# ScalarE's queue in the seven-product down layers: program order in place of the scheduler's order

## The chip, the cores and the metric

The kernel runs on one NeuronCore of one Trainium2 chip. The metric is device time of one execution in microseconds (us). Three runs of the kernel before gave 905.02, 900.41 and 902.4 us: a median of 902.4.

The engines are named as the profile names them: PE is TensorE (matmul) and PEld its weight loads, DVE is VectorE, ACT is ScalarE, POOL is GpSimd, SP is the engine that issues most of the DMAs. Each engine works off its own queue of instructions, and semaphores hold an instruction back until what it needs is done.

## The reference

Two stages, in float32. First an attention within chunks of 64 positions (batch 8, 8 heads, 576 positions, head dimension 64): for every chunk, `softmax(q k^T / 8) v`. The result is laid out as `x` with 4608 tokens of 512 features. Then a gated feed-forward layer:

```
gate = 1 / (1 + exp(-(x @ w_gate)))     # 512 -> 1536
val  = x @ w_val                        # 512 -> 1536
out  = (gate * val) @ w_out             # 1536 -> 512
```

## The kernel before

The 4608 tokens are nine blocks of 512. Float32 operands are split in two float32r parts, a high part (a cast on ACT) and a low part (value minus high part, on DVE); each product then takes three matmuls (weight high with data high, weight high with data low, weight low with data high), always in this order.

Blocks 0 to 2 go through plain up and down layers. The other six blocks go in three pairs, n = 0, 1, 2. A pair is computed as a 2 by 2 block product with seven products in place of eight (a Winograd form), once for the up layers (`first`, `middle`, `last`, lines 518 to 568) and once for the down layer (`down_begin`, `down_products`, lines 644 to 718). Blocks 1 and 2 share the down layer too, as pair n = -1.

A down layer walks through 42 spots: seven products r in the order 1, 6, 2, 7, 5, 4, 3, with six slices f each (`SPOTS`, line 573). A spot is six matmuls of 512 columns. Before its matmuls run, its data must be split: `down_split` (lines 625 to 642) casts the high part on ACT (line 640, into tiles `hs` and `hx`) and subtracts the low part on DVE (line 641). Splits are issued three spots ahead in pairs -1, 0 and 1, and six ahead in pair 2. Spots 0, 1 and 4, 5 and so on lie two to a tile `hs` of which there is one; spots 2, 3 and 6, 7 and so on lie in two tiles `hx`. So the cast of spot q + 4 has to wait until the matmuls of the spots that used the same tile are done.

In between (`between`, lines 928 to 936), with each spot of pairs -1, 0 and 1, the operands of the next pair's up layers are prepared from its attention output `raw` (`operands`, `lower`, lines 476 to 499). There are seven, named B11, B22, T1, T3, B21, T2, T4. For each, ACT casts 1024 columns (`xc`, line 489) and DVE subtracts the low part (line 498). The four named T need a difference of two quarters of `raw` first, made on DVE in place (line 485). The casts of B11, B22 and B21 need no such difference.

The rest of the work in a down layer is the reading of finished banks: on ACT lines 674 and 682, on DVE lines 686 and 689, and the sums for later products on DVE (lines 617 to 621, 705).

What sets the order of an engine's queue: inside `tc.manual_schedule(engines=...)` the named engines take instructions in the order in which the code issues them. Engines that are not named are put in order by a scheduler, which moves an instruction forward or back by its own estimate of when its inputs are there. Lines 942 to 951 name PE, DVE, SP and POOL for all pairs, and ACT for `singles()` and `pair(-1)`.

Of the kernel before, what the change touches and what calls it, by code (L numbers as in the profile page):

```python
# [42 lines left out]
FIRST_PAIR = 3  # L43
# [10 lines left out]
def chunk_attn_moe(ctx: ExitStack, tc: tile.TileContext, q, k, v, w, out, turned_out):  # L54
# [377 lines left out]
    def place(n):  # L432
        rotation.append(rotation.pop(0))
        return wp.tile([P, n], F32R, tag=rotation[-1], name="wr")
# [3 lines left out]
    def load_group(n, p, which, parts=(0, 1)):  # L438

        def of_given(t, n):  # L440
            return lambda a, c: t[:, n * 512 + a * 256 + c * P:n * 512 + a * 256 + (c + 1) * P]
        def of_sums(t, n):
            return lambda a, c: t[:, n * 512 + c * 256 + a * P:n * 512 + c * 256 + (a + 1) * P]
        lhs = groups.setdefault((n, p, which), {})
        for part in parts:
            g, g0, s = ((2, 0, slice(0, 4, 3)), (1, 2, slice(1, 3)))[part]
            t = place((g + 2) * 512)
            if p < RESIDENT:
                nc.sync.dma_start(
                    t[:, :g * 512].rearrange("p (g n) -> p g n", g=g).bitcast(F32),  # L450
                    given[p, which][:, g0:g0 + g].rearrange("p g a n -> p g (a n)"))
            else:
                of_given = of_sums
                for k in range(g):
                    nc.sync.dma_start(
                        t[:, k * 512:(k + 1) * 512].rearrange("p (c a n) -> p c a n", c=2, a=2).bitcast(F32),
                        whole[p, which][:, part, :, (part + k)::2])
            nc.sync.dma_start(
                t[:, g * 512:].rearrange("p (s n) -> p s n", s=2).bitcast(F32),
                sums[p, which][:, s].rearrange("p s c n -> p s (c n)"))  # L460
            if part == 0:
                lhs.update({
                    1: (of_given(t, 0), "B11"), 2: (of_given(t, 1), "B21"), 6: (of_sums(t, 2), "T2"),
                    5: (of_sums(t, 3), "T1")})
            else:
                lhs.update({4: (of_given(t, 0), "T4"), 3: (of_sums(t, 1), "B22"), 7: (of_sums(t, 2), "T3")})
# [36 lines left out]
    def product(n, p, which, r, bank, start, stop):  # L503
        lhs, name = groups[n, p, which][r]
        x, k = xc[n, name], 0
        for c in range(2):
            for wpart, part in ((0, 0), (0, 1), (1, 0)):
                nc.tensor.matmul(  # L508
                    bank, lhsT=lhs(wpart, c), rhs=x[:, part, c], start=start and k == 0, stop=stop and k == 5,
                    skip_group_check=True)  # L510
                k += 1
# [6 lines left out]
    def first(n, p, which):  # L518
        x = ps_o.tile([P, TB], F32, tag="acc", name="cx")
        y = ps_o.tile([P, TB], F32, tag="acc", name="cy")  # L520
        product(n, p, which, 1, x, True, True)
        both = mp.tile([P, 2, TB], F32, tag="hx", name="s1")
        s1, u2 = both[:, 0], both[:, 1]
        nc.scalar.copy(s1, x)  # L524
        product(n, p, which, 6, y, True, True)
        nc.vector.tensor_tensor(out=u2, in0=y, in1=s1, op=ALU.add)  # L526
        banks[n, p, which] = x, y, s1, u2

    def gated(n, f, b, value):

        h = hid[n, f][:, b]
        nc.vector.tensor_tensor(out=h, in0=value, in1=h, op=ALU.mult)
# [21 lines left out]
    def last(n, p, which):  # L554
        y, z, s1, u2 = banks.pop((n, p, which))
        f = 2 * p
        product(n, p, which, 4, y, False, True)
        c21 = hid[n, f + 1][:, 0] if which == 0 else s1
        nc.vector.tensor_tensor(out=c21, in0=y, in1=s1, op=ALU.add)
        product(n, p, which, 3, z, False, True)  # L560
        c12 = hid[n, f][:, 1] if which == 0 else u2
        nc.vector.tensor_tensor(out=c12, in0=z, in1=u2, op=ALU.add)
        if which == 0:
            nc.scalar.activation(hid[n, f + 1], hid[n, f + 1], AF.Sigmoid)
            nc.scalar.activation(hid[n, f][:, 1], hid[n, f][:, 1], AF.Sigmoid)
        else:
            gated(n, f + 1, 0, s1)
            gated(n, f, 1, u2)
# [75 lines left out]
    def down_begin(n):  # L644

        ring["splits"], *ring["weights"] = rotation
        rotation[:] = rotation[4:] + rotation[1:4] + rotation[:1]
        for i in range(2):
            load_down(n, i)
        for q in range(3 if n < LAST else 6):  # L650
            down_split(n, q)
# [136 lines left out]
    def advance():  # L788
        now["unit"] += 2 * (now["item"] == "A")
        now["item"] = next(ahead, None)  # L790
        now["since"] = now["ticks"]

    def tick(share):
        now["ticks"] += 1
        now["credit"] += share
        while now["item"] is not None:
            if isinstance(now["item"], float):
                if now["credit"] < now["item"] / 2:
                    return
                now["credit"] -= now["item"]  # L800
            elif not (now["item"] == "wait" and now["ticks"] > now["since"] + 1
                      or now["item"] == "next" and now["ticks"] > now["since"]
                      or now["item"][0] in ("open", "freed") and now["item"][1] <= now[now["item"][0]]):
                break
            advance()
        now["credit"] = min(now["credit"], share)

    def insert(upto=4 * NB, pieces=0):


        if now["item"] == "S" or (
                now["item"] == "A" and now["unit"] < upto and now["ticks"] >= now["since"] + pieces):
            advance()

    def due(n):

        while now["item"] is not None and len([x for x in xc if x[0] == n]) < 7:
            advance()
# [47 lines left out]
    def keep(n=1):  # L866
        for _ in range(n):
            if kept:
                keep_sums(*kept.pop(0))
# [29 lines left out]
                if kept[0][2] is None:  # L899
                    keep()  # L900

    def pair(n):
        m0 = FIRST_PAIR + 2 * n
        upto = 4 * (m0 + 4)
        order = [(p, which) for p in range(6) for which in range(2)]
        if n >= 0:
            due(n)
        for i, (p, which) in enumerate(order if n >= 0 else ()):
            if i + 1 < len(order) and i > 0:
                load_group(n, *order[i + 1])  # L910
            first(n, p, which)
            tick(SHARES["up"])
            if i:
                keep(2)
                last(n, *order[i - 1])
                tick(SHARES["up"] if i < 11 else 0)
                insert(upto, 1)
                if i > 1:
                    down_sums(n, i - 2)
            middle(n, p, which)  # L920
            tick(SHARES["up"] if i < 11 else 0)
            insert(upto, 1)
        if n >= 0:
            down_begin(n)
            last(n, *order[-1])
        now["open"] = n + 1

        def between(q):
            now["freed"] = q if n < 0 else 99
            if n < LAST:  # L930
                if q in (32, 36):
                    load_group(n + 1, 0, 0, ((q - 32) // 4,))
                if n < 0 and q == 32:
                    fetch(*kept[0], nc.sync)
                tick(SHARES["turned"] if q > 3 else 0)
                insert(upto, 1)

        down_products(n, between)
        if n < LAST:
            load_group(n + 1, 0, 1)  # L940

    with tc.manual_schedule(engines={mybir.EngineType.PE}):
        with tc.manual_schedule(engines={mybir.EngineType.SP}):
            for op in MIDDLE.split():
                run(op)
        with tc.manual_schedule(engines={mybir.EngineType.DVE, mybir.EngineType.SP, mybir.EngineType.Pool}):
            with tc.manual_schedule(engines={mybir.EngineType.Activation}):
                singles()
                pair(-1)
            for n in range(3):  # L950
                pair(n)


# [29 lines left out]
```

## Time and profile before

| | |
|---|---|
| median of three runs | 902.4 us |
| profiled execution | 902.69 us |
| span of its trace | 900.9 us (1.79 us lie around it) |
| mean granted TensorE clock | 0.996 |
| busy share of the span | PE 97%, DVE 75%, ACT 44%, POOL 27% |

A row of the timeline gives the start, the duration of the merged instructions, engine, line of the kernel, operation, output and input, shapes, and a count; in brackets stands how long the engine was idle before it, and what ended the idle time. A PE row of twelve matmuls is two spots; its duration is longer than the distance to the next row's start, as matmuls overlap, so distances between starts are what counts. On ACT and DVE too an instruction's write-back overlaps with the next instruction.

In the trace, pair -1's down layer lies at 297 to 358 us, pair 0's at 485 to 543, pair 1's at 667 to 725 and pair 2's at 839 to 897, and the up layers of the pairs lie between.

### The profile page before, as it was taken

How to read it: one execution, taken by the hardware profiler on the slowest of the kernel's cores; microseconds unless marked ns; L12 is line 12 of the kernel's file. 1: busy time of each engine (PE TensorE's matmuls, PEld its weight loads, DVE VectorE, ACT ScalarE, POOL GpSimd, SP SyncE). 2: the span in 40 equal slices, each digit the busy share in tenths (PEclk: the TensorE clock that was granted, in tenths of full speed). 3: DMA queues.
4: the chain of work that ended last, by engine and by line, in shares of the span. 5: the costliest groups of instructions: out<-in, count | busy, mean ns of one | idle time of the engine just before them, and what ended most of it. 6: DMA issues, size and time to landing. Idle time of an engine off the chain costs nothing.

```text
span 900.9 us, 15584 instructions
## 1 busy us (share of the span) xinstructions
PE 870.1 (97%) x6016; PEld 714.7 (79%) x6016; DVE 671.9 (75%) x1007; ACT 397.7 (44%) x734; POOL 240.0 (27%) x275
## 2 busy tenths in 40 slices
PE   4799999999999899999999999999999999999998
PEld 3687889888877687887887888878878888888886
DVE  6999954566877778787897895777778945656973
ACT  6989642334444544234436542442345511122540
POOL 0111127998993002898820000000000000000000
PEclk9999999999999899999999999999999999999999
DMA  8786686699676666999977678595565785564772
GB/s 317 271 273 215 196 272 223 226 332 379 247 255 194 190 208 230 369 326 365 367 255 221 192 231 280 181 297 167 187 196 179 228 276 197 182 206 150 233 211 94
DMA packets 152107, 216.53 MB, mean 240 GB/s; under 512 B 9056, under 2 KB 90464, under 8 KB 150496
## 3 DMA queue, kind: packets, MB, share of 16 engines
q1 hardware_dynamic: 143248, 178.29, 61.3%
q0 software_dynamic: 8784, 37.23, 10.9%
q8 instruction: 48, 0.79, 0.4%
q14 instruction: 27, 0.22, 0.1%
HBM read 169.87 MB, written 45.61 MB: 239 GB/s over the span
## 4 chain that ended last, share of the span: by engine, by line
PE 63%; DMA 2%; ACT 1%; SPq 1%; DVE 1%; issue 0%; ACTq 0%
PE dx L665 18%; PE cy L508 15%; PE cz L508 11%; PE cx L508 10%; PE dz L665 7%; DMA wr<-sums 2%; PE av L248 1%; PE sc L177 1%; SPq L148 1%; DVE hx L641 0%; ACT hx L640 0%; ACT xc L489 0%; DVE hid L689 0%; ACT hs L640 0%; DVE raw L485 0%
## 5 line engine op out<-in xcount | busy, mean ns | idle before, releaser
L508 PE MATMUL cy<-xc,wr 128*128 128x512 f32 x648 | 159.3, 389 | 0.6 <-DMA wr<-sums 0.6
L508 PEld LDWEIGHTS cy<-xc,wr 128*128 128x128 f32 x648 | 121.5, 188 | 26.7 <-DVE mx L746 1.4
L282 PE MATMUL acc<-xt,w 128*128 128x512 f32 x480 | 112.6, 393 | 0.0
L508 PE MATMUL cz<-xc,wr 128*128 128x512 f32 x432 | 107.3, 392 | 0.0
L508 PE MATMUL cx<-xc,wr 128*128 128x512 f32 x432 | 106.0, 391 | 1.2 <-DMA wr<-given 1.2
L665 PE MATMUL dx<-hs,wd 128*128 128x512 f32 x432 | 104.6, 397 | 2.7 <-ACT hs L640 2.7
L282 PEld LDWEIGHTS acc<-xt,w 128*128 128x128 f32 x480 | 89.1, 188 | 18.9
L665 PEld LDWEIGHTS dx<-hs,wd 128*128 128x128 f32 x432 | 82.6, 191 | 20.8 <-ACT hs L640 3.1
L282 PE MATMUL g<-xt,w 128*128 128x256 f32 (+1 forms) x528 | 94.4, 334 | 4.7 <-ACT xt L268 2.1
L508 PEld LDWEIGHTS cx<-xc,wr 128*128 128x128 f32 x432 | 80.6, 188 | 18.4 <-DMA wr<-given 1.6
L508 PEld LDWEIGHTS cz<-xc,wr 128*128 128x128 f32 x432 | 80.3, 188 | 16.9
L282 PEld LDWEIGHTS g<-xt,w 128*128 128x128 f32 x528 | 80.3, 190 | 15.8 <-ACT xt L268 2.7
L665 PE MATMUL dx<-hx,wd 128*128 128x512 f32 x288 | 70.8, 393 | 0.5 <-DVE hx L641 0.5
L665 PEld LDWEIGHTS dx<-hx,wd 128*128 128x128 f32 x288 | 54.2, 189 | 13.4 <-DVE hx L641 1.7
L526 DVE TENSOR_TENSOR s<-cy,s 128x512 f32<-128x512 f32 x36 | 24.9, 692 | 51.7 <-PE cy L508 45.8
L524 ACT COPY s<-cx 128x512 f32<-128x512 f32 x36 | 21.2, 589 | 83.4 <-PE cx L508 81.1
L640 ACT CAST hs<-hid 128x512 fp32r<-128x512 f32 x66 | 38.3, 620 | 44.3 <-PE dx L665 27.2
L641 DVE TENSOR_TENSOR hs<-hid,hs 128x512 fp32r<-128x512 f32 x66 | 43.6, 702 | 14.4 <-ACT hs L640 14.4
L665 PE MATMUL dz<-hs,wd 128*128 128x512 f32 x216 | 51.3, 389 | 0.0
L363 POOL DMA_DIRECT2D outer<-w x24 | 18.6, 773 | 115.0 <-DVE w L136 46.4
L548 ACT ACTIVATE hid<-cx 128x512 f32<-128x512 f32 x18 | 10.8, 598 | 83.5 <-PE cx L508 83.4
L665 PEld LDWEIGHTS dz<-hs,wd 128*128 128x128 f32 x216 | 40.5, 188 | 8.4
(135 smaller groups left out, 1417.7 us busy)
## 6 DMA issues: line engine op xcount, KB each, us to landing
wr<-sums SPq DMA_DIRECT2D x72, 512.0 KB, 6.3
w_raw<-w_in SPq DMA_DIRECT2D x36, 512.0 KB, 5.2
wd<-outer SPq DMA_DIRECT2D x72, 256.0 KB, 5.6
wd<-outer_sums SPq DMA_DIRECT2D x16, 1024.0 KB, 6.2
wr<-whole SPq DMA_DIRECT2D x54, 256.0 KB, 4.5
qt<-q_in SPq DMA_DIRECT2D x36, 256.0 KB, 4.5
kt<-k_in SPq DMA_DIRECT2D x36, 256.0 KB, 4.8
vt<-v_in SPq DMA_DIRECT2D x36, 256.0 KB, 4.2
```

The costliest lines, as they stand in the source:

```text
L148: nc.sync.dma_start(t, src[2 * m + h, u].rearrange("p (a n) -> p a n", a=2))
L177: nc.tensor.matmul(sc[i][half * D:(half + 1) * D, n0:n0 + D], lhsT=x[rows, a, chunk], rhs=y[rows, a, chunk], start=True, stop=True)
L248: nc.tensor.matmul(av[c][a * D:(a + 1) * D, n0:n0 + D], lhsT=vt[u][rows, i, a, t, :], rhs=pt[rows, i, u, t, a, :], start=True, stop=True)
L282: nc.tensor.matmul(ps[:, tok], lhsT=wt[f, which][:, wpart, c:c + P], rhs=xt[m][:, part, 2 * u + i, tok], start=n == 0, stop=n == 11)
L363: nc.gpsimd.dma_start(outer[:, f, c], src[:, :, c])
L508: nc.tensor.matmul(bank, lhsT=lhs(wpart, c), rhs=x[:, part, c], start=start and k == 0, stop=stop and k == 5, skip_group_check=True)
L524: nc.scalar.copy(s1, x)
L526: nc.vector.tensor_tensor(out=u2, in0=y, in1=s1, op=ALU.add)
L548: nc.scalar.activation(hid[n, f][:, 0], x, AF.Sigmoid)
L640: nc.scalar.copy(hi, src)
L641: nc.vector.tensor_tensor(out=lo, in0=src, in1=hi.bitcast(F32), op=ALU.subtract)
L665: nc.tensor.matmul(bank[to][c], lhsT=down_lhs(r, f, wpart, c), rhs=down_in[q][part], start=r in (1, 6, 5) and (f, i) == (0, 0), stop=stop ...
```

## The change

`pair(n)` is cut in two functions: `pair_up(n)` issues the up layers, `pair_down(n)` the down layer with the last quarter of the up layers' work. The calls for n = 0, 1, 2 now put `pair_down(n)` under `manual_schedule` for ACT. The up layers of these pairs stay with the scheduler. The instructions are the same ones.

```diff
-    def pair(n):
-        m0 = FIRST_PAIR + 2 * n
-        upto = 4 * (m0 + 4)
-        order = [(p, which) for p in range(6) for which in range(2)]
-        if n >= 0:
-            due(n)
-        for i, (p, which) in enumerate(order if n >= 0 else ()):
-            if i + 1 < len(order) and i > 0:
-                load_group(n, *order[i + 1])
+    ORDER = [(p, which) for p in range(6) for which in range(2)]
+
+    def pair_up(n):
+        upto = 4 * (FIRST_PAIR + 2 * n + 4)
+        due(n)
+        for i, (p, which) in enumerate(ORDER):
+            if i + 1 < len(ORDER) and i > 0:
+                load_group(n, *ORDER[i + 1])
             first(n, p, which)
...
             middle(n, p, which)
             tick(SHARES["up"] if i < 11 else 0)
             insert(upto, 1)
+
+    def pair_down(n):
+        upto = 4 * (FIRST_PAIR + 2 * n + 4)
         if n >= 0:
             down_begin(n)
-            last(n, *order[-1])
+            last(n, *ORDER[-1])
         now["open"] = n + 1
...
             with tc.manual_schedule(engines={mybir.EngineType.Activation}):
                 singles()
-                pair(-1)
+                pair_down(-1)
             for n in range(3):
-                pair(n)
+                pair_up(n)
+                with tc.manual_schedule(engines={mybir.EngineType.Activation}):
+                    pair_down(n)
```

The queues of PE, DVE, POOL and SP keep their order; on ACT the instructions of the three down layers of pairs 0, 1 and 2 stand otherwise. The next three pieces are of ACT's queue.

At the start of pair 0's down layer (a minus is before, a plus after; `hs` and `hx` are the split casts of the spots, `xc` an operand of the next pair, `t_4103` a tile that is split later):

```order
 L265 COPY raw<-av 128x4x2x64 x2
-L640 CAST hx<-hid 128x512
+L640 CAST hx<-hid 128x512 x2
 L489 CAST xc<-raw 128x1024 x2
-L640 CAST hs<-hid 128x512
-L640 CAST hx<-hid 128x512
-L640 CAST hs<-hid 128x512
+L640 CAST hs<-hid 128x512 x2
 L640 CAST hx<-t_4103 128x512 x2
```

The cast for spot 3 (the second `hx`) moves ahead of the two `xc` casts, and the casts for spots 4 and 5 (`hs`) now stand together behind them. The two `xc` are B11 and B22 now; before they were B21 and B22, and B11 stood further ahead, among the up layers' instructions.

Further on in the same layer, from the split of spots 10 and 11 (`hx` of `t_4850`) on; before:

```order
L640 CAST hx<-t_4850 128x512 x2
L640 CAST hs<-hid 128x512
L489 CAST xc<-raw 128x1024
L640 CAST hs<-hid 128x512
L640 CAST hx<-hid 128x512 x2
L640 CAST hs<-hid 128x512 x2
L640 CAST hx<-hid 128x512 x2
L682 COPY obs<-dx 128x512
L489 CAST xc<-raw 128x1024
L640 CAST hs<-hid 128x512
L682 COPY obs<-dx 128x512
L640 CAST hs<-hid 128x512
```

and the same place after:

```order
L640 CAST hx<-t_4850 128x512 x2
L489 CAST xc<-raw 128x1024
L640 CAST hs<-hid 128x512 x2
L640 CAST hx<-hid 128x512 x2
L640 CAST hs<-hid 128x512 x2
L640 CAST hx<-hid 128x512
L489 CAST xc<-raw 128x1024
L640 CAST hx<-hid 128x512
L640 CAST hs<-hid 128x512
L682 COPY obs<-dx 128x512 x2
L640 CAST hs<-hid 128x512
L489 CAST xc<-raw 128x1024
```

The cast of T1 moves ahead of spot 12's cast, and the cast of T3 ahead of spot 19's (the second `hx<-hid` of its pair); the third `xc`, of B21, comes here from the start of the layer.

For spots 28 and 29 (`hs` of `t_4103`) in the same layer:

```order
-L640 CAST hs<-t_4103 128x512 x2
+L640 CAST hs<-t_4103 128x512
+L489 CAST xc<-raw 128x1024
+L640 CAST hs<-t_4103 128x512
 L640 CAST hx<-t_4103 128x512 x2
-L489 CAST xc<-raw 128x1024
 L640 CAST hs<-t_4850 128x512 x2
 L640 CAST hx<-t_4850 128x512 x2
```

The cast of T2 moves from behind spot 31's cast to between those of spots 28 and 29. Then, behind these rows, the cast of T4 moves in the same way from behind spot 37's cast to ahead of spot 36's. Pair 1's down layer has the same moves as pair 0's. Pair 2's has no `xc`; there, copies of line 674 and 682 and split casts change places among themselves.

## Rows read from the trace of the kernel before

**Rows 1.** Busy time by stretch: us from and to, length, then busy time and count of PE, PEld, DVE, ACT and POOL, granted clock, DMA share, GB/s. The first is the start of pair -1's down layer, the others are the down layers of pairs 0, 1 and 2.

```profile
297.00:304.00 7.00, 6.71 (x16) 5.00 (x17) 5.63 (x8) 4.16 (x8) 0.00 (x0) 0.52 0.57 156
485.00:543.00 58.00, 57.77 (x254) 47.15 (x253) 51.22 (x75) 29.44 (x48) 0.00 (x0) 1.00 0.76 231
667.00:725.00 58.00, 57.77 (x254) 47.17 (x253) 51.22 (x75) 29.44 (x48) 0.00 (x0) 1.00 0.66 211
839.00:897.00 58.00, 57.79 (x255) 47.51 (x254) 39.66 (x66) 20.33 (x36) 0.00 (x0) 1.00 0.61 183
```

**Rows 2.** Timeline of PE in pair 0's down layer; the last row is the first of the next up layers.

```profile
485.25 2.88 PE L665 MATMUL dx<-hs,wd 128*128 128x512 f32 x12
487.97 1.90 PE L665 MATMUL dx<-hx,wd 128*128 128x512 f32 x7
490.09 1.40 PE L665 MATMUL dx<-hx,wd 128*128 128x512 f32 x5 [0.23 <-DVE hx L641]
491.33 2.88 PE L665 MATMUL dx<-hs,wd 128*128 128x512 f32 x12
...
515.81 3.09 PE L665 MATMUL dx<-hx,wd 128*128 128x512 f32 x12
518.74 2.88 PE L665 MATMUL dz<-hs,wd 128*128 128x512 f32 x12
...
524.18 2.88 PE L665 MATMUL dz<-hs,wd 128*128 128x512 f32 x12
...
535.06 2.88 PE L665 MATMUL dz<-hs,wd 128*128 128x512 f32 x12
...
543.22 1.52 PE L508 MATMUL cx<-xc,wr 128*128 128x512 f32 x6
```

**Rows 3.** Timeline of PE at the same place of pair 1's down layer, and the first two thirds of pair 2's.

```profile
670.01 1.94 PE L665 MATMUL dx<-hx,wd 128*128 128x512 f32 x7
...
673.43 2.88 PE L665 MATMUL dx<-hs,wd 128*128 128x512 f32 x12
...
839.51 32.80 PE L665 MATMUL dx<-hs,wd 128*128 128x512 f32 x144
```

**Rows 4.** Timeline of ACT in pair 0's down layer.

```profile
485.51 1.05 ACT L489 CAST xc<-raw 128x1024 fp32r<-128x1024 f32 x1 [1.72 <-PE cz L508]
488.17 0.62 ACT L640 CAST hs<-hid 128x512 fp32r<-128x512 f32 x1 [1.61 <-PE dx L665]
488.70 0.61 ACT L640 CAST hx<-hid 128x512 fp32r<-128x512 f32 x1
...
500.22 1.05 ACT L489 CAST xc<-raw 128x1024 fp32r<-128x1024 f32 x1
501.17 0.61 ACT L640 CAST hs<-hid 128x512 fp32r<-128x512 f32 x1
```

**Rows 5.** Timeline of DVE in pair 0's down layer.

```profile
487.11 1.28 DVE L532 TENSOR_TENSOR hid<-s,hid 128x512 f32<-128x512 f32 x2
489.35 0.69 DVE L641 TENSOR_TENSOR hx<-hid,hx 128x512 fp32r<-128x512 f32 x1 [0.96 <-ACT hx L640]
489.96 1.28 DVE L641 TENSOR_TENSOR hs<-hid,hs 128x512 fp32r<-128x512 f32 x2
...
498.46 1.22 DVE L485 TENSOR_TENSOR raw<-raw 128x1024 f32<-128x1024 f32 x1
...
501.81 0.69 DVE L641 TENSOR_TENSOR hs<-hid,hs 128x512 fp32r<-128x512 f32 x1 [0.77 <-ACT hs L640]
...
508.97 1.22 DVE L485 TENSOR_TENSOR raw<-raw 128x1024 f32<-128x1024 f32 x1
510.11 0.68 DVE L641 TENSOR_TENSOR hx<-hid,hx 128x512 fp32r<-128x512 f32 x1
...
513.03 0.69 DVE L641 TENSOR_TENSOR hs<-hid,hs 128x512 fp32r<-128x512 f32 x1 [0.32 <-ACT hs L640]
...
523.22 1.22 DVE L485 TENSOR_TENSOR raw<-raw 128x1024 f32<-128x1024 f32 x1
524.35 0.68 DVE L641 TENSOR_TENSOR hs<-t,hs 128x512 fp32r<-128x512 f32 x1
...
531.50 1.22 DVE L485 TENSOR_TENSOR raw<-raw 128x1024 f32<-128x1024 f32 x1
```

**Rows 6.** Timelines of ACT, then DVE, then PE at the end of pair -1's down layer, whose ACT instructions stand in program order before and after.

```profile
352.12 1.05 ACT L489 CAST xc<-raw 128x1024 fp32r<-128x1024 f32 x1 [3.14 <-DVE raw L485]
353.07 0.61 ACT L640 CAST hx<-hid 128x512 fp32r<-128x512 f32 x1
...
350.82 1.21 DVE L485 TENSOR_TENSOR raw<-raw 128x1024 f32<-128x1024 f32 x1
353.72 0.69 DVE L641 TENSOR_TENSOR hx<-hid,hx 128x512 fp32r<-128x512 f32 x1 [1.69 <-ACT hx L640]
...
352.23 2.01 PE L665 MATMUL dz<-hx,wd 128*128 128x512 f32 x7
355.73 2.91 PE L665 MATMUL dz<-hs,wd 128*128 128x512 f32 x12
```

**Rows 7.** Timeline of PE at the start of pair -1's down layer.

```profile
297.29 5.79 PE L665 MATMUL dx<-hs,wd 128*128 128x512 f32 x12 [2.69 <-ACT hs L640]
```

**Rows 8.** Timeline of ACT in pair 2's down layer: the wait for a sum that stands among the split casts.

```profile
846.89 0.62 ACT L640 CAST hs<-t 128x512 fp32r<-128x512 f32 x1 [0.55 <-DVE t L620]
```

More of the change, by code (lines that the diff above doesn't have):

```diff
@@ L914, in pair @@
                 keep(2)
-                last(n, *order[i - 1])
+                last(n, *ORDER[i - 1])
                 tick(SHARES["up"] if i < 11 else 0)
```

## The prediction

> **What bounds the kernel now.** I read first the busy time by stretch: in each of the three down layers PE is busy 57.8 of 58 us at a granted clock of 1.00, DVE 51.22 us in pairs 0 and 1, ACT 29.44 [rows 1]. So PE sets the time, and DVE stands close behind it. Second, the timeline of PE, by distances between starts: two spots without a halt take 2.72 us (485.25 to 487.97), so a spot takes 1.36 us and a matmul 0.227 [rows 2]. The 42 spots of a layer need 57.12 us; pair 0's took 543.22 - 485.25 = 57.97. The 0.85 us lie at two places: 487.97 to 491.33 is 0.64 too long, 515.81 to 518.74 is 0.21 too long [rows 2]. In pair 1 the first place loses 0.70; pair 2 shows 144 matmuls in one piece with no loss [rows 3]. There is thus little to win in these layers, some 1.7 us in all, and what can change the time is a new wait of PE. Third, I read who holds PE at 490.09: the low part of spot 3, whose cast on ACT came late [rows 2, 4, 5].
>
> **The links of the chain**, from rows. A cast of 512 columns lets the next one on ACT start 0.53 us later (488.17 to 488.70) and ends after 0.62; an `xc` cast holds ACT for 0.95 (500.22 to 501.17) [rows 4]. DVE starts 0.04 after the cast ends (488.70 + 0.61, then 489.35), a low part takes 0.69 and the next follows 0.60 after its start [rows 4, 5]. PE starts 0.05 after the low part ends (489.35 + 0.69, then 490.09); from there five matmuls should take 1.13 us, and the next spot began 0.11 later than that (491.33), so a halt costs 0.11 on top [rows 2, 5]. Within a spot the second matmul already needs the low part. ACT starts 0.09 after the difference of line 485 ends (350.82 + 1.21, then 352.12) [rows 6].
>
> **The change part by part.** Nothing is added or removed; only ACT's order differs, and the queues of PE, DVE, POOL and SP stand as they did, so no DMA is issued in another order. What can go: spot 3's cast. Its tile is free when the two line 532 instructions end at 487.11 + 1.28 = 488.39 [rows 5]; it can start at 488.42 in place of 488.70 [rows 4], so 0.28 of the 0.64 goes. What comes late next is at five places of pair 0, each an `xc` cast that now stands before a split. Before, these casts stood behind it and so in ACT's idle time.
>
> Place A, spot 4. Behind spot 3's cast stand B11 and B22: 488.42 + 0.53 + 0.95 + 0.95 = 490.85 for spot 4's cast (before: 488.17 [rows 4]). It ends at 491.47, its low part runs 491.51 to 492.20 on DVE (before 489.96 [rows 5]), the second matmul starts at 492.25. Five matmuls and 0.11 on: 493.49, where spot 5 began at 491.33 + 1.36 = 492.69 before [rows 2]. PE is 0.80 later, what spot 3 gained included.
>
> Place B, spot 12, behind T1. Its difference on DVE came 498.46 - 489.96 = 8.50 after spot 4's low part, with DVE at work nearly throughout [rows 5]; so now 500.01 to 501.23. T1's cast starts at 501.32, spot 12's at 502.27 and ends at 502.89; low part 502.93 to 503.62; matmul 503.67. It would have been due at 491.33 + 8 x 1.36 + 0.23 + 0.80 = 503.24. PE loses 0.43 + 0.11 and is 1.34 late. DVE's next low part is at 503.53, in place of 501.81 [rows 5]: 1.72 late.
>
> Place C, spot 19, behind T3. Difference 508.97 + 1.72 = 510.69 [rows 5], ends 511.91; T3 512.00, spot 19's cast 512.95, ends 513.57; low part 513.61 (before 510.11 [rows 5]) to 514.30; matmul 514.35. Due 491.33 + 15 x 1.36 + 0.23 + 1.34 = 513.30. PE loses 1.05 + 0.11, 2.50 late. Behind it on ACT come spot 20's cast, two copies of a bank and spot 21's cast, costed at 0.53 each: 515.07, its low part 515.73, 2.70 later than 513.03 [rows 5]. DVE waited 0.32 there before and more ahead of it, so part of its delay is made up.
>
> B21's cast, which comes next on ACT, waits for no difference; spots 22 and 23 follow it, and I leave the 0.21 which PE lost there before as it is.
>
> Place D, spot 29, behind T2. Difference 523.22 + 2.70 = 525.92 [rows 5], ends 527.14; T2 527.23, spot 29's cast 528.18 to 528.80; low part 528.84 (before 524.35 [rows 5], so 4.49 late) to 529.53; matmul 529.58. Due 524.18 + 1.36 + 0.23 + 2.50 = 528.27 [rows 2]. PE loses 1.31 + 0.11, 3.92 late.
>
> Place E, spot 36, behind T4. Difference 531.50 + 4.49 = 535.99 [rows 5], ends 537.21; T4 537.30, cast 538.25 to 538.87; low part 538.91 to 539.60; matmul 539.65. Due 535.06 + 0.23 + 3.92 = 539.21 [rows 2]. PE loses 0.44 + 0.11: 4.47 late at the end of the layer.
>
> Nothing hides this: the up layers behind it are bound by PE as well, and their operands come with the same delay as PE. Pair 1 has the same order and the same busy times (57.77, 51.22, 29.44) [rows 1], so it costs 4.5 again. Pair 2 has no `xc`; its casts run six spots ahead. In program order spot 10's cast waits for a sum until 846.89 [rows 8], and is due at 839.51 + 13.6 = 853.1 [rows 3], 6 us of cover; I cost it at 0, and if that cover were gone it would be one place like the others, about 1 us. The sum is 2 x 4.47 = 8.9, on the profiled execution's 902.69 us: 911.6, and I say 911.5. The profiled execution lies 0.3 us from the median of 902.4, so the sum holds for the median too.
>
> **Bounds.** The trace has one place of this kind on the chip: in pair -1, already in program order, an `xc` waits 3.14 us for its difference, the split behind it holds DVE idle for 1.69, and PE takes 355.73 - 352.23 = 3.50 for 2.72, a loss of 0.78 [rows 6]. Five places at 0.78, less the 0.64 that could go, twice: +6.5, so 909.2. Five at the whole of DVE's 1.69 in the same way: +15.6, so 918.3. My five losses, with the 0.28 that A gains taken out, average 0.95: between the ends and nearer to the one measured loss, 0.78.
>
> **Rivals.** First, no change that can be measured: DVE makes up its delay in its 58 - 51.22 = 6.8 us of idle time [rows 1], and each difference runs when it did before. From a difference's start to the matmul takes 1.22 + 0.09 + 0.95 + 0.62 + 0.04 + 0.69 + 0.05 = 3.66. The four began 3.98, 2.99, 2.55 and 3.79 ahead of their second matmul [rows 2, 5], so only C (0.67) and D (1.11) would halt PE, and with B11 and B22 done early A would not either: with 0.11 each and without the 0.64, +1.4 a pair, 905.4. For it speaks the idle time; against it that DVE's idle time lies where it waits for ACT, which the change makes longer. The Trainium skill speaks for this side too, in "Perfetto Trace Analysis", section Identifying the Most-Contended Engine: the engine with the highest occupancy is the one to work on. By that rule ACT's order would be worth nothing and the time stay 902.7. The 0.78 of pair -1 speaks against it, since ACT was far from full there.
>
> Second, on the other side, a gain: all `xc` casts find their differences done, and spot 3's halt goes wholly, from the point where spot 3's cast is early enough (0.64 us earlier than now). Then 902.69 - 0.64 - 0.70 = 901.3. Against it: the tile of that cast is not free before 488.39 [rows 5], and place A has two `xc` in a row.
>
> Third, PE's clock falls. After PE waited 2.69 us at 297.29 [rows 7], the granted clock was 0.52 until 304, so mostly the lower level of 1.2 GHz, and 16 matmuls took 6.71 us in place of 3.63: 3.1 lost [rows 1]. My halts are under 1.3 us, and the 0.78 of pair -1 brought no such row; but they come five to a layer. One fall in each pair would give 911.5 + 6.2 = 917.7. The Trainium skill, "TensorE: Matmul & The Clock Gate", section A second HAM failure mode: psum-queue depth-cycling, tells of a kernel whose frequent short halts of PE made the clock swing between its levels. By that rule this rival would be the likely one; the 1.00 of pair 0's layer with two halts [rows 1] does not bear it out so far.
>
> **How the numbers follow.** The forecast has 0.74, no change 0.14, the gain 0.04, the clock 0.08. A difference under 0.5% (4.5 us) can't be told from none. The forecast's own range, a quarter of its 8.9 us to each side, is 909.3 to 913.7, all of it over the 906.9 at which slower begins (902.4 + 4.5); its tail below that is some 0.02, so with the clock case slower is 0.80. The gain of 1.4 us would count as the same for the most part, so same is 0.18 and 0.02 is left for faster. The range runs from 904.5, below the no-change case, to 916, short of two falls of the clock and of the upper bound.
>
> **What would show it.** Right: in pair 0's down layer PE rows with halts at spots 4, 12, 19, 29 and 36, each ended by ACT `hs` or DVE `hs` or `hx`; DVE idle before line 641 some 1.6 us right after line 485; the layer near 62.4 us long, pair 1's alike, pair 2's 57.1. Wrong: a layer of 58 to 59 us, or `xc` rows on ACT without a wait for line 485, or a granted clock under 1.00 between 485 and 550.

## The result, and the profile after

The changed kernel took 908.05 to 911.2 us in four runs, with a median of 911.0 us, beside 902.35 us for four runs of the kernel before. The ratio, estimated from all these runs, is 1.0086, with a 95% interval from 1.0072 to 1.0100 (the two medians alone give 1.0096): slower by 0.9%, and by more than the 0.5% that can be told from no change. The profiled execution took 911.0 us, with a span of 909.2 us at a mean granted clock of 0.997. Two executions of kernels further down ran at a low granted clock from end to end (1341.47 us at 0.603 in best_before, 1243.23 us at 0.652 in best_late); they are left out of the medians and ratios there.

First the page's busy times. They hardly show the loss: PE 96% (97% before), DVE 74% (75%), ACT 43% (44%), and the counts of these engines are the same.

```profile
PE 873.2 (96%) x6016; PEld 712.6 (78%) x6016; DVE 673.4 (74%) x1007; ACT 395.2 (43%) x734; POOL 241.8 (27%) x275
```

The busy times by stretch answer to [rows 1]; the columns are the same. The windows of pairs 0 and 1 are 62 us long now, since the layers are. Line by line they are the start of pair -1's layer and the layers of pairs 0, 1 and 2.

```profile
297.00:304.00 7.00, 4.50 (x12) 3.38 (x13) 6.46 (x8) 4.18 (x7) 0.00 (x0) 0.76 0.70 215
485.00:547.00 62.00, 60.13 (x254) 46.71 (x253) 51.85 (x76) 30.60 (x50) 0.00 (x0) 1.00 0.74 223
671.00:733.00 62.00, 60.21 (x254) 46.74 (x253) 51.24 (x75) 30.59 (x50) 0.00 (x0) 1.00 0.64 198
847.00:905.00 58.00, 58.00 (x257) 47.84 (x255) 40.04 (x65) 19.21 (x36) 0.00 (x0) 1.00 0.60 185
```

The same 254 matmuls of [rows 1] need four microseconds more in pairs 0 and 1, at the same granted clock of 1.00. Pair 2's layer keeps its length.

The timeline of PE in pair 0's layer shows where, and answers to [rows 2]; the last row is the first of the next up layers.

```profile
486.23 2.88 PE L665 MATMUL dx<-hs,wd 128*128 128x512 f32 x12
488.95 3.28 PE L665 MATMUL dx<-hx,wd 128*128 128x512 f32 x12
492.49 0.50 PE L665 MATMUL dx<-hs,wd 128*128 128x512 f32 x1 [0.26 <-ACT hs L640]
...
495.89 2.88 PE L665 MATMUL dx<-hx,wd 128*128 128x512 f32 x12
...
504.05 3.22 PE L665 MATMUL dx<-hs,wd 128*128 128x512 f32 x12
507.11 2.88 PE L665 MATMUL dx<-hx,wd 128*128 128x512 f32 x12
...
512.55 1.52 PE L665 MATMUL dx<-hx,wd 128*128 128x512 f32 x6
514.32 0.49 PE L665 MATMUL dx<-hx,wd 128*128 128x512 f32 x1 [0.25 <-ACT hx L640]
515.05 1.45 PE L665 MATMUL dx<-hx,wd 128*128 128x512 f32 x5 [0.23 <-DVE hx L641]
516.33 2.90 PE L665 MATMUL dx<-hs,wd 128*128 128x512 f32 x12
...
527.46 1.52 PE L665 MATMUL dz<-hs,wd 128*128 128x512 f32 x6
529.35 0.49 PE L665 MATMUL dz<-hs,wd 128*128 128x512 f32 x1 [0.37 <-ACT hs L640]
...
531.34 2.88 PE L665 MATMUL dx<-hx,wd 128*128 128x512 f32 x12
...
539.50 0.40 PE L665 MATMUL dz<-hs,wd 128*128 128x512 f32 x1
540.09 2.77 PE L665 MATMUL dz<-hs,wd 128*128 128x512 f32 x11 [0.19 <-DVE hs L641]
542.70 2.94 PE L665 MATMUL dz<-hx,wd 128*128 128x512 f32 x12
...
548.20 1.52 PE L508 MATMUL cx<-xc,wr 128*128 128x512 f32 x6
```

Again distances between starts count. 486.23 to 548.20 is 61.97 us, where the layer took 57.97 before. Spot 19 shows the pattern of a long halt: its first matmul waits for the cast (ACT), and the second then waits for the low part (DVE). From 512.55, spot 18 should take 1.36 and took 1.77; the first matmul of spot 19 should take 0.23 and took 0.73; the remaining five took 1.28 in place of 1.13. Taken two or more spots at a time against 1.36 each, the rows lose 1.50 at spots 3 and 4 (488.95 to 495.89), 0.34 at spot 12 (504.05 to 507.11), 1.06 at spot 19 (512.55 to 516.33) and 0.02 in the row behind it, 1.16 at spot 29 (527.46 to 531.34) and 0.48 at spot 36 (539.50 to 542.70). With 0.23 at spot 22 and 0.06 at spot 39 that is the 4.85 by which the layer exceeds the 57.12 of its 42 spots.

What ACT waits for is in the view of line 489 (idle time in us before its casts in the whole trace, and how often). First the row of the kernel before, then that of the changed one: the casts waited 5.3 us for a difference of line 485, twice, and now 27.4 us, ten times.

```profile
  DVE raw L485: 5.3, 2
...
  DVE raw L485: 27.4, 10
```

The timelines of ACT and of DVE around place C show how that wait travels on.

```profile
512.70 1.05 ACT L489 CAST xc<-raw 128x1024 fp32r<-128x1024 f32 x1 [3.41 <-DVE raw L485]
513.65 0.61 ACT L640 CAST hx<-hid 128x512 fp32r<-128x512 f32 x1
...
511.45 1.22 DVE L485 TENSOR_TENSOR raw<-raw 128x1024 f32<-128x1024 f32 x1
514.30 0.69 DVE L641 TENSOR_TENSOR hx<-hid,hx 128x512 fp32r<-128x512 f32 x1 [1.63 <-ACT hx L640]
```

T3's cast waits 3.41 us on ACT for the difference, with spot 19's cast behind it in the queue. The difference ends at 512.67, the `xc` cast starts at 512.70, the split cast at 513.65, and DVE, which has nothing else to do in its order, sits idle for 1.63 us before the low part. PE follows at 515.05. Before, DVE made this low part right behind the difference [rows 5].

Where the 8.3 us of span went (909.2 - 900.9): 4.00 in pair 0's layer (61.97 - 57.97), 3.97 in pair 1's (61.95 - 57.98), nothing in pair 2's (57.12 both times). The rest, 0.98 in what runs ahead of pair 0's layer, -0.59 in the up layers between pairs 0 and 1 and -0.1 at the end, is in parts whose instructions are the same. These parts scatter from run to run. The changed kernel is already 1.39 us behind at a PE wait near 164 us that every trace has (163.53 before, 164.92 now), far ahead of the change, and the up layers between pairs 0 and 1 took from 123.5 to 124.5 us in the traces of this study. The layers of pairs 0 to 2 repeat to about 0.06 us where their order is the same; pair -1's, with a stretch of lower clock at its start, does not. So the experiments below are read by the lengths of these down layers. A single time tells little: 17 runs of the kernel before, taken together, lay between 901.16 and 908.14 us.

### The profile page after: what moved, and what is told of

Its sections match the earlier page's. It is cut to its first block, busy times and chain, and to the rows that moved or that the text cites. A ratio compares the mean times of both kernels' runs of the same rounds, so it can differ in the third digit from the quotient of the medians.

```text
span 909.2 us, 15603 instructions
## 1 busy us (share of the span) xinstructions
PE 873.2 (96%) x6016; PEld 712.6 (78%) x6016; DVE 673.4 (74%) x1007; ACT 395.2 (43%) x734; POOL 241.8 (27%) x275
## 4 chain that ended last, share of the span: by engine, by line
PE 68%; DVE 16%; ACT 8%; DMA 3%; issue 3%; SPq 1%; ACTq 0%; DVEq 0%
PE cy L508 15%; PE dx L665 13%; PE cz L508 10%; PE cx L508 10%; PE g L282 7%; PE dz L665 5%; PE acc L319 3%; PE acc L282 2%; DVE hs L641 2%; DVE hx L641 1%; PE av L248 1%; PE sc L177 1%; DVE hid L309 1%; DVE sums L773 1%; DMA wr<-given 1%
```

## The experiments

The theory is the prediction's: an `xc` cast that stands ahead of a split cast holds it back, by the wait for its difference (where it has one) and by its own 0.95 us. The rivals were that DVE's order or load sets the loss, that the split casts' own program order does, or that it lies in the clock. In the traces of the first five runs below, DVE's 1007 rows stand in the same order, by line and tile, as in those of the kernels before and after, so none of these runs changes DVE's queue. All lengths below are distances between starts of PE rows in us; the pairs' columns are the lengths of the down layers.

| kernel | start of -1 | pair -1 | pair 0 | pair 1 | pair 2 |
|---|---|---|---|---|---|
| before | 297.29 | 61.18 | 57.97 | 57.98 | 57.12 |
| after | 299.27 | 60.09 | 61.97 | 61.95 | 57.12 |
| xc_scheduled | 298.73 | 59.88 | 58.30 | 58.32 | 57.12 |
| t_scheduled | 299.88 | 60.19 | 59.02 | 59.00 | 57.12 |
| pair1_scheduled | 297.41 | 61.23 | 61.95 | 58.00 | 57.12 |
| late2 | 298.24 | 59.78 | 60.57 | 60.57 | 57.12 |
| diff_late2 | 300.44 | 59.38 | 58.44 | 58.49 | 57.12 |
| best_before | 295.93 | 59.37 | 58.01 | 58.03 | 57.12 |
| best_late_b | 296.82 | 57.12 | 58.49 | 58.45 | 57.12 |

**The `xc` casts alone.** In the layers of pairs 0 and 1 the seven `xc` casts go back to the scheduler; all other instructions of ACT stay in program order (`freed` closes the manual schedule around one instruction).

```diff
-            nc.scalar.copy(t[:, 0], at)
+            with freed(True):
+                nc.scalar.copy(t[:, 0], at)
```

> The changed kernel, with the seven xc casts of a pair alone handed back to the scheduler; splits and bank copies of the down layers stay in program order. Theory (the place of the xc casts costs the 8.6 us): the layers of pairs 0 and 1 go back from 62.0 to about 58 us, the time to 902.4 within 2. Rival (the new order of splits and copies costs it, the xc casts only wait along): the layers stay near 62, the time near 911.

Measured: 904.51 us (median of 10 runs), ratio 1.0015 with an interval from 0.9999 to 1.0031, so no difference from before that can be told; layers of 58.30 and 58.32. Of the 4.00 us per layer, 3.67 go with these seven casts, and the program order of the split casts and copies costs at most the 0.33 that is left. Most of that part sits at spot 22, which loses 0.49 here (0.21 before).

**The four with a difference.** Only the casts of T1, T3, T2 and T4 go back to the scheduler; B11, B22 and B21 stay in program order.

```diff
-            nc.scalar.copy(t[:, 0], at)
+            with freed(less):
+                nc.scalar.copy(t[:, 0], at)
```

> The changed kernel, with the casts of T1, T3, T2 and T4 alone handed back to the scheduler; B11, B22 and B21 stay in program order. Theory: places B to E (spots 12, 19, 29, 36) lose nothing, place A (spots 3 and 4) keeps its 0.38 + 1.04 us; with 0.2 at spot 22 a layer takes 58.7 to 58.8, the time is 902.4 + 1.6 = 904. Rival (B11 and B22 at the start set DVE back and the later places only follow from it): places C to E keep most of their loss and the layer stays over 60.5.

Measured: 906.05 us in one run; layers of 59.02 and 59.00. The timeline of PE has no halt left at spots 12, 19, 29 and 36; the one at spot 4 stands.

```profile
492.60 0.50 PE L676 MATMUL dx<-hs,wd 128*128 128x512 f32 x1 [0.26 <-ACT hs L651]
```

(In this kernel and in xc_scheduled lines from 489 on stand 11 further on.) So the four T cost 61.97 - 59.02 = 2.95 us per layer and the three B 59.02 - 58.30 = 0.72: 0.80 more at spots 3 to 5, 0.08 less at spot 22.

**One pair alone.** The change for pairs 0 and 2; pair 1's layer goes back to the scheduler whole.

```diff
-                with tc.manual_schedule(engines={mybir.EngineType.Activation}):
+                with ExitStack() as held:
+                    if n != 1:
+                        held.enter_context(tc.manual_schedule(engines={mybir.EngineType.Activation}))
                     pair_down(n)
```

> The change for pairs 0 and 2 alone, pair 1's down layer left to the scheduler. Theory (a fixed loss per layer with xc casts, none for pair 2): pair 0's layer 62.0, pair 1's 58.0, pair 2's 57.1; the time 902.4 + 4.2 = 906.6. Rival (the loss comes once, for the change of the queue as a whole, or pair 2 has a share): another split of the layers' lengths, a time over 909 or under 904.

Measured: 906.2 us in one run; layers of 61.95, 58.00 and 57.12. Each layer's loss belongs to its own order; nothing of pair 0's delay reaches pair 1, and pair 2's new order costs nothing.

**The preparation two spots later.** ACT in program order throughout; B11 and what follows it may be issued only from spot 2 on.

```diff
-        now["open"] = n + 1
+        if n < 0:
+            now["open"] = 0
...
         def between(q):
             now["freed"] = q if n < 0 else 99
+            if q == 2:
+                now["open"] = max(now["open"], n + 1)
```

> The changed kernel, with the operand preparation of pairs 0 and 1 opened at spot 2 in place of spot 0, so that B11 and B22 stand behind the casts of spots 4 and 5: place A is undone, the casts of the four T stay ahead of their splits. Theory (each place costs by its own wait): spot 4 loses nothing, C, D and E keep about 1.1, 1.2 and 0.6, B next to nothing, with 0.4 at spot 3 and 0.3 at spot 22 a layer takes 60.7; the time is 902.4 + 2 x 2.8 = 908. Rival (all follows from place A): the layer goes back to 58, the time to 902.5.

Measured: 907.29 us in one run; both layers 60.57. B11 and B22 now stand behind the casts of spots 4 and 5, and place A is gone, but so is B: T1's cast no longer holds PE up. Spots 19, 29 and 36 still lose 1.05, 1.12 and 0.48, spot 3 0.42 and spot 22 0.29. At spot 19 the timelines of ACT and DVE show the picture of the changed kernel:

```profile
510.35 1.05 ACT L489 CAST xc<-raw 128x1024 fp32r<-128x1024 f32 x1 [3.42 <-DVE raw L485]
511.31 0.61 ACT L640 CAST hx<-hid 128x512 fp32r<-128x512 f32 x1
...
509.10 1.22 DVE L485 TENSOR_TENSOR raw<-raw 128x1024 f32<-128x1024 f32 x1
511.95 0.69 DVE L641 TENSOR_TENSOR hx<-hid,hx 128x512 fp32r<-128x512 f32 x1 [1.63 <-ACT hx L640]
```

The step buys 61.97 - 60.57 = 1.40 us per layer, 1.05 of it at spots 3 to 5 and 0.32 at spot 12. T1's cast still stands ahead of spot 12's, so place B hangs on place A: a delay at the start reaches the difference behind it.

**The cast one spot behind its difference.** late2, and in addition each T's cast is issued one spot after the subtraction. It was meant to find its difference done when ACT comes to it; it still stands ahead of a split cast with its 0.95 us, but of the next one. (The pairs' lines behind 485 stand one further on.)

```diff
                 nc.vector.tensor_tensor(out=at, in0=raw[n][:, u0, :, b0], in1=raw[n][:, u1, :, b1], op=ALU.subtract)
+                yield "next"
```

> The kernel of the run late2 (operand preparation opened at spot 2), and each T's cast is issued one spot after its difference in place of right behind it, so that the difference is done when ACT comes to the cast; all in program order still. Theory (what PE waits for is the difference on DVE, handed on by ACT): places C, D and E go, a layer of pairs 0 and 1 falls from 60.6 to 58.0 to 58.4 us, ACT shows no xc row that waits over 1 us for line 485; time near 903. Rival (an xc cast in front of a split is enough, by the 0.95 us for which it holds ACT): the layers stay over 60 us, the time near 907.

Measured: 904.83 us in one run; layers of 58.44 and 58.49. The three halts that late2 had left are gone. The timelines of ACT and of DVE at the same place:

```profile
511.67 1.05 ACT L490 CAST xc<-raw 128x1024 fp32r<-128x1024 f32 x1 [1.75 <-DVE raw L485]
512.62 0.61 ACT L641 CAST hs<-hid 128x512 fp32r<-128x512 f32 x1
...
510.41 1.22 DVE L485 TENSOR_TENSOR raw<-raw 128x1024 f32<-128x1024 f32 x1
511.55 0.68 DVE L642 TENSOR_TENSOR hx<-hid,hx 128x512 fp32r<-128x512 f32 x1
513.26 0.69 DVE L642 TENSOR_TENSOR hs<-hid,hs 128x512 fp32r<-128x512 f32 x1 [1.03 <-ACT hs L641]
```

The `xc` cast still waits, 1.75 us (T2's waits 1.57), where no wait over 1 us was expected, and it stands in front of a split cast. But spot 19's low part comes right behind the difference (510.41, 511.55), since its cast was done before, and the split that stands behind the `xc` cast is one spot further from its due time. DVE still sits idle for 1.03 us, and PE does not notice. So it is not the wait of the cast by itself that costs: the place of the cast in the queue relative to the next due split makes the loss, with ACT in program order and the same instructions on all engines. What is left is 0.40 at spot 3, 0.49 at spot 22 and 0.41 at spot 33.

**The loss that both kernels share.** The longest single wait of PE in these layers is in neither part of the change: 2.69 us at the start of pair -1's layer [rows 7]. It has the same form. ACT's timeline in the kernel before has three `xc` casts ahead of the first split casts:

```profile
292.04 1.99 ACT L489 CAST xc<-raw 128x1024 fp32r<-128x1024 f32 x2
295.68 1.04 ACT L489 CAST xc<-raw 128x1024 fp32r<-128x1024 f32 x1 [1.65 <-issue]
296.63 1.13 ACT L640 CAST hs<-hid 128x512 fp32r<-128x512 f32 x2
```

So in the kernel before, the first three splits of pair -1 are issued one step earlier, and the last two steps of block 2 issue no operand preparation.

```diff
-                if m == 2 and f == NF - 1:
+                if m == 2 and f == NF - 2:
                     down_begin(-1)
                 step(m, f, "", True)
-                tick(SHARES[m])
+                tick(SHARES[m] if m < 2 or f < 10 else 0)
                 insert(upto, 1)
                 if m == 2 and f < NF - 2:
                     down_sums(-1, f)
-                tick(SHARES[m])
+                tick(SHARES[m] if m < 2 or f < 10 else 0)
```

> The kernel before, with the same mechanism taken out of the start of pair -1's down layer: its first three splits are issued one step earlier (step 10 of 12 of block 2), and the operand preparation gets no ticks in steps 10 and 11, so that no xc cast stands in front of the first splits. Theory: PE's pause of 2.69 us at 297 goes, with it the stretch at the lower clock; of the layer's 4.06 us 0.8 to 1.6 are left. Gain 2.69 + 4.06 - 1.2 = 5.5, the time 897. Rival (the xc casts come later and stand before other splits, and their work has to be done before pair 0 begins): the gain is under 2 us, 900.5 or more.

Measured: 899.43 us (median of 11 runs), ratio 0.9955 with an interval from 0.9939 to 0.9971: faster by 0.45%, some 4.1 us, and not by the 5.5 expected. The pause is gone and with it the stretch at a lower clock; which of the two edits does it, no run tells. Timelines of ACT and PE, then busy times by stretch:

```profile
291.62 1.15 ACT L640 CAST hs<-hid 128x512 fp32r<-128x512 f32 x2
...
295.93 2.88 PE L665 MATMUL dx<-hs,wd 128*128 128x512 f32 x12
...
297.00:304.00 7.00, 7.00 (x32) 5.79 (x32) 6.18 (x11) 3.48 (x7) 0.00 (x0) 1.00 0.97 284
```

Part of the gain is given back inside the same layer. It takes 59.37, not 57.12: spots 9 and 16 lose 0.88 and 0.57 now, and spot 39 its 0.78 as before. The edit has moved the preparation into the layer: T1's difference ran at 294.37 before, 2.92 us ahead of the layer's start, and runs at 305.55 now, 9.62 us behind it. Spot 9's row on ACT is another T cast in front of a split:

```profile
306.80 1.05 ACT L489 CAST xc<-raw 128x1024 fp32r<-128x1024 f32 x1 [0.92 <-DVE raw L485]
307.76 0.61 ACT L640 CAST hs<-t 128x512 fp32r<-128x512 f32 x1
...
309.15 1.42 PE L665 MATMUL dx<-hs,wd 128*128 128x512 f32 x5 [0.23 <-DVE hs L641]
```

**Both together.** diff_late2 with the two edits of best_before, ACT in program order in all layers.

> The kernel of the run diff_late2 with the start of pair -1's down layer as in best_before: all down layers in program order, every T's cast one spot after its difference, also in pair -1. Theory: pair -1's layer loses next to nothing (57.1 to 57.5), its pause before goes, pairs 0 and 1 take 58.0 to 58.4: 902.4 - 2.69 - 4.06 + 2 x 0.3 = 896.2. Rival (program order costs by itself, wherever the xc casts stand): over 900.

Measured: 898.25 us (median of 5 runs), ratio 0.9939 with an interval from 0.9915 to 0.9962. The same kernel was run again for its trace.

> The same kernel as best_late, to see its stages in a trace at the full granted clock. Theory (the start of the layer of the pair before the first costs about 2 us more when PE pauses before it, and the later places of the casts cost about 0.4 us in each of the layers of pairs 0 and 1): that layer at 57.1 to 59.4 us, the next two at 58.4 each, the last at 57.1, no pause of 2.7 us at its start; a span of 896 to 898 us. Rival (what the start gains is lost again behind the later casts): the first layer at 60 or more, the next two at 59 or more, a span above 900.

Measured: 898.92 us (median of 6 runs), ratio 0.9956 with an interval from 0.9937 to 0.9975; span 897.9. The timeline of PE shows pair -1's layer in spots without a halt from its first row to its last, and then pair 0's layer with its first loss, at spot 3:

```profile
296.82 2.88 PE L666 MATMUL dx<-hs,wd 128*128 128x512 f32 x12
...
353.94 1.52 PE L509 MATMUL cx<-xc,wr 128*128 128x512 f32 x6
...
480.67 2.88 PE L666 MATMUL dx<-hs,wd 128*128 128x512 f32 x12
483.39 3.28 PE L666 MATMUL dx<-hx,wd 128*128 128x512 f32 x12
486.51 2.88 PE L666 MATMUL dx<-hs,wd 128*128 128x512 f32 x12
```

353.94 - 296.82 = 57.12, the 42 spots at 1.36 exactly: the one-spot distance between difference and cast works in pair -1 as well, at spots 9, 16 and 39. Program order with this distance and with the earlier start of pair -1 beats both kernels. Whether it beats best_before, whose layers of pairs 0 and 1 are 0.4 to 0.5 us shorter each and whose pair -1 is 2.25 longer, the intervals do not tell.

## Why the prediction came out as it did

The forecast of 911.5 us, measured 911.0, rests on the right mechanism: halts at the five places A to E, ended by DVE's low part (at A, C and D the first matmul already waits for ACT; at B the halt is too short for the view to name what ended it), DVE idle for 1.63 to 1.72 us before line 641, pair 1 like pair 0, a granted clock of 1.00. Pair 2 lost nothing, as its cover held: spot 10's cast started at 855.31, due at 847.87 + 13.6 = 861.5. The experiments that take the casts away, one group at a time, take the halts away with them. Part of the nearness is luck: the layers cost 4.00 + 3.97 = 7.97 us where 8.9 was predicted, and scatter elsewhere added 0.3.

Term by term, by distances between rows, net of what was lost before at spot 3:

| place | predicted | measured in pair 0 |
|---|---|---|
| A, with spot 3's gain | 0.80 | 0.86 |
| B | 0.54 | 0.34 |
| C | 1.16 | 1.08 |
| spot 22, more than the 0.21 before | 0 | 0.02 |
| D | 1.42 | 1.16 |
| E | 0.55 | 0.48 |
| spot 39 | 0 | 0.06 |
| sum | 4.47 | 4.00 |

**Place A** came out to the row. Spot 3's cast was put at 488.42 and spot 4's at 490.85; with the layer's start 0.98 us later that is 489.40 and 491.83, and the timeline of ACT has 489.40 and 491.82. One sentence of the prediction is wrong here, that the `xc` casts stood behind the split before: at this place `xc` casts stood ahead of it, the last at 485.51 [rows 4], in ACT's idle time. In program order spot 3's cast stands first, waits 7.84 us for line 532, and holds both `xc` casts back until they come right before spot 4's:

```profile
489.40 0.62 ACT L640 CAST hx<-hid 128x512 fp32r<-128x512 f32 x1 [7.84 <-DVE hid L532]
489.93 1.99 ACT L489 CAST xc<-raw 128x1024 fp32r<-128x1024 f32 x2
491.82 1.13 ACT L640 CAST hs<-hid 128x512 fp32r<-128x512 f32 x2
```

**Places B to E** were mis-sized upward by two terms. One is the link from the difference to its cast: 0.09 was read from pair -1 [rows 6], and here it is 0.03 (511.45 + 1.22 = 512.67, cast at 512.70), so some 0.06 too much at each place. The other is DVE's delay, carried on almost whole from place to place: the four differences were predicted 1.55, 1.72, 2.70 and 4.49 us later than before, and stand 1.40, 1.50, 2.28 and 4.00 later (500.84, 511.45, 526.48 and 536.48, less the 0.98 by which the layer starts later). DVE made up some of it, as the text at C said it would without a number for it; at D that alone is 0.42. Part of this cancels, since a PE that is less late needs its low part sooner: at E the difference stood 0.49 nearer than predicted, and the loss shrank by 0.07 only.

**The bounds.** Five places at pair -1's 0.78 gave 909.2, the nearer end; the layers' 7.97 on 902.69 make 910.7, between that end and the forecast.

**The rival that DVE makes up its delay** was wrong by its premise: it needed the differences to run when they did before. DVE has the idle time, but sits in it waiting for ACT behind its own difference. The Trainium skill's rule in "Perfetto Trace Analysis", Identifying the Most-Contended Engine, is to optimize the engine with the highest occupancy first. The prediction's reading of it, that ACT's order would then be worth nothing, is not borne out by the trace: ACT was busy 30.60 of 62 us, and its order cost 4 us of them.

**The rival of a gain** failed at both of its conditions. The casts of T1 to T4 did not find their differences done (in this layer they waited 2.17 to 3.41 us for them), and spot 3's halt did not go wholly: of its 0.64, 0.39 stayed, so 0.25 went, near the 0.28 of the forecast. Place A's two casts took that back, as its text held against it.

**The rival of the clock** did not come: 1.00 through both layers, with halts of PE at seven spots in each (3, 4, 12, 19, 22, 29 and 36). The Trainium skill tells in "TensorE: Matmul & The Clock Gate", A second HAM failure mode: psum-queue depth-cycling, of one kernel whose frequent short halts made the clock swing between its levels. Taken as a rule, as the prediction took it, that would have had the clock swing here; the rows of the changed kernel show no such swing, for halts of at most 0.53 us between one matmul and the next.

Some expectations behind the prediction failed in size. best_before was put at 5.5 us faster and gave 4.1: the pause and the lower clock went, but the sum left 1.2 us of loss in pair -1's layer, and 2.25 stayed, 1.45 of them at spots 9 and 16. best_late was expected lower by about 2 us than it came. Layers of 57.12, 58.49 and 58.45 answer for some 0.4 of this. The trace of best_late_b is 1.87 us behind that of the kernel before at the wait near 164 us (165.40 beside 163.53), ahead of every edit, so much of the rest may be scatter; that is not shown for the other runs. xc_scheduled and t_scheduled came some 2 us above the times expected, with layers within 0.3 us of the lengths expected.

## What to carry to other kernels

In an engine's queue in program order, an instruction that waits for another engine holds up everything behind it, so look for work of no urgency that stands with such a wait ahead of work that the bounding engine needs soon; its price is the whole chain from the other engine's result to the matmul, less the lead that the chain had. Before handing the order to a scheduler, try one step of distance between the producer and its consumer on the other engine: here it took away 2.1 us per layer (60.57 to 58.44) with no other edit, though in these two layers the scheduler's order stayed 0.5 us shorter (57.97). Judge such edits of a microsecond by the lengths of stages that repeat to some hundredths in the trace, not by single times.

## What the runs showed of the hardware that was not expected

The same wait at the start of pair -1's layer, 2.68 to 2.71 us in each of the seven traces that have it, was followed by a different length of lower clock. Over the 7 us from the layer's start the granted clock was 0.55 in the kernel before and 0.54 in pair1_scheduled, where the layer took 61.18 and 61.23 us; it was 0.76 in the other five, where the layer took from 59.38 to 60.19 us. (In these stretches a mean below 1.00 is a mix of the clock's lower level, 1.2 GHz, and the full 2.4 GHz.) A wait at another place did so in one trace and not in another: in xc_scheduled PE waited 2.56 us for a DMA at 410.19, and the stretch behind it had a granted clock of 0.72; in the changed kernel, with 1.64 us of wait there, it stayed at 1.00. The timeline of PE and the busy times of that stretch, first of xc_scheduled:

```profile
410.19 1.84 PE L519 MATMUL cx<-xc,wr 128*128 128x512 f32 x6 [2.56 <-DMA wr<-given]
...
410.00:416.00 6.00, 5.81 (x18) 4.40 (x19) 1.19 (x3) 2.73 (x6) 5.28 (x9) 0.72 1.05 388
```

and of the changed kernel:

```profile
410.00 1.66 PE L508 MATMUL cx<-xc,wr 128*128 128x512 f32 x6 [1.64 <-DMA wr<-given]
...
410.00:416.00 6.00, 6.00 (x36) 4.54 (x40) 4.12 (x6) 2.83 (x7) 5.53 (x9) 1.00 1.05 391
```

In these six microseconds PE started 18 matmuls of 512 columns in xc_scheduled, and 24 and some small ones of the attention in the changed kernel. How much of the scatter of single times comes from such stretches was not measured.
